# Both heads' exponentials of 512 queries in one instruction, from two-bank score tiles

## The chip, the cores and the metric

The kernel runs on one core of a Trainium2 chip. That core has a matrix engine (TensorE, PE in the profile, with its weight loads listed as PEld), a vector engine (VectorE, DVE), an engine for functions such as the exponential (ScalarE, ACT), a general one (GpSimd, POOL) and SyncE (SP), which here only starts DMAs. The metric is the device time of one execution in microseconds (us). The results of matrix multiplications go to PSUM, a small memory of eight banks; a bank holds 512 float32 numbers in each of 128 partitions. ScalarE and VectorE read the results from there.

## What is computed

Two branches are mixed by a gate: softmax attention with 32 heads of 16 numbers over 2048 positions, and a Fourier mixing made of matrix products.

```python
# x: 2048 x 512
g = sigmoid((x * gate_w).sum(-1, keepdims=True))
q, k, v = (x @ wqkv) split into 32 heads of 16
p = softmax(q @ k.T * 16 ** -0.5)          # per head, 2048 x 2048
a = (p @ v, heads joined) @ wo
b = dft_seq_re @ (x @ dft_hid_re.T) - dft_seq_im @ (x @ dft_hid_im.T)
out = g * a + (1 - g) * b
```

## The kernel before

**The front.** The first part projects x to q, k and v, computes the Fourier branch, and also runs 564 of the 1024 "scans". A scan (`scan`, L110) computes the scores of 128 queries against 512 keys for the two heads of a head pair, and VectorE takes the row maxima of both heads in one reduction (L121). The maxima become a shift that is added inside the score product later, so that the exponentials do not overflow. The front is not touched by the change.

**The attention part** (from L506) works through the 16 head pairs in `NP * PERIODS` = 512 steps, 32 for each pair p. A step takes one block `kb` of 128 keys and one half `h` of the queries (1024 of 2048), and treats it as two score pairs, c = 0 and c = 1, of 512 queries each. The two heads j = 0, 1 of a head pair sit in partitions 0 to 49 and 64 to 113, and their two score products are issued one after the other into different banks, and run beside each other in the two halves of TensorE's rows. I call the two products of c = 0 pair A of a step and those of c = 1 pair B.

`qk2` (L523) does one score pair: it takes a tile `e` in SBUF (six buffers), two PSUM tiles, issues the two products (L530) and then the exponentials (L533) from PSUM into `e`. `pv` (L538) multiplies the four quarters of a step's `e` with the values; its four products write four groups of 32 partitions of the one bank `pvb`, and each appears as two MATMUL records. `pvb` accumulates over 16 steps, is copied out by VectorE (L545), and is divided later on GpSimd (`divide`, L552).

**The order on TensorE** is written out by the loop at L721. In a step n from 1 to 460 it is: pair A of step n; a scan of a later head pair, into the two-bank tile `s1`, which has one buffer; pair B of step n; `pv` of step n-1. TensorE executes this in order, so an instruction that waits holds up all that follows.

The 1024 scans are used up after step 460. From step `MIX` = 461 to 511 the scans' place is taken by the output projection: `outputs()` (L675) hands out pieces of it, one for each step, in tile `s1`, whose accumulated products VectorE adds to the output (`take_in`, L626). In an odd step the piece comes after pair B, and no `pv` is issued; in an even step it comes between pair A and pair B, and then both pending `pv` follow. Two such steps form a cycle: A, B, piece, A, piece, B, `pv`, `pv`. A piece is counted in steps of two products that run beside each other. By the argument of `mix_heads` in L679 the pieces of a cycle have 2 and 2, or 2 and 3, for token blocks 0, 2 and 4 (six cycles), and 4 and 5 for the other thirteen blocks; then `mix_some` (L661) gives three cycles of 3 and 3 and three of 3 and 6. The rest of the output products (L764 to L807) come after step 511, from banks that are taken by `part` (L690) and by `spread` (L772).

**PSUM.** The attention part uses all eight banks: one for `pvb`, two for the tile `s1`, and five single-bank tiles `s2` that `bank()` hands out in rotation. A score product may write a bank when the exponential that read it last is done: with five banks that is the fifth exponential back. An exponential waits for its product; `pv` waits for the exponentials of its step. These waits are semaphores, and the wait of a product stands on its weight load.

Of the kernel before, what the change touches and what calls it, by code (L numbers as in the profile page):

```python
# [10 lines left out]
F32 = mybir.dt.float32  # L11
F32R = mybir.dt.float32r
AF = mybir.ActivationFunctionType
# [5 lines left out]
P = 128  # L19
# [9 lines left out]
SCALE = DH ** -0.5  # L29
# [12 lines left out]
def build(tc, x, xT, wqkv, wo, wrT, wiT, cr, ci, gate, out):  # L42
    nc = tc.nc
    with ExitStack() as ctx:
# [105 lines left out]
        with ExitStack() as pf:  # L150
# [32 lines left out]
            def beside():  # L183

                slots[0] += 1
                run_due()
                if pace[0] is None:
                    return
                pace[1] += 1.0 / pace[0]
                while seen[0] < FRONT and pace[1] >= 1.0:  # L190
                    pace[1] -= 1.0
                    n = seen[0]
                    if n % SCANS == 36:
                        load_scan_beside(n // SCANS + 1)
                    scan(n, s1())
                    seen[0] += 1
                    if seen[0] % SCANS == 0:
                        for d, part in enumerate(shift(n // SCANS)):
                            after(3 + 4 * d, part)
# [234 lines left out]
            with ExitStack() as py:  # L434
# [11 lines left out]
                pss, yre, early = {}, {}, {}  # L446
# [59 lines left out]
        with ExitStack() as pa:  # L506
            ps2 = pa.enter_context(tc.tile_pool(name="ps2", bufs=1, space=PSUM, reuse_waits="tile"))
# [4 lines left out]
            pvb = ps2.tile([P, 512], F32, tag="pv", name="pvb")  # L512
# [4 lines left out]
            def pair_banks():  # L517
                return ps2.tile([P, 2, 512], F32, tag="s1", name="s1")

            def bank():  # L520
                return ps2.tile([P, 512], F32, tag="s2", name="s2", bufs=5)

            def qk2(p, h, kb, c):  # L523
                e = pr.tile([P, 2, 512], F32, tag="e", name="e")
                q0 = h * 1024 + c * 512
                qs, ks = used[p]
                pss = [bank() for j in range(2)]
                for j in range(2):
                    b = 64 * j
                    nc.tensor.matmul(pss[j], ks[b:b + 50, kb * P:(kb + 1) * P],  # L530
                                     qs[b:b + 50, q0:q0 + 512], start=True, stop=True)
                for j in range(2):
                    nc.scalar.activation(e[:, j, :], pss[j], AF.Exp, scale=SCALE)  # L533
                return e

            quads = [(c, j, 64 * c + 32 * j) for c in range(2) for j in range(2)]
# [114 lines left out]
            def mix_rest(t, ps, k, first, last):  # L651

                h, q = t // 8, slice((t % 4) * P, (t % 4 + 1) * P)
                for n, (a, b) in enumerate(((0, 0), (0, 1), (1, 0))):
                    halves_of(ps, direct[h][k][a][:, q], w4[k][b], first and n == 0, last and n == 2)
# [32 lines left out]
            groups = {}  # L688

            def part(t, *ks):  # L690

                if t not in groups:
                    groups[t] = (bank(), pvb) if t == 11 else (bank(), bank())
                    if t in (3, 8):
                        ps = pair_banks()
                        groups[t] = ps[:, 0, :], ps[:, 1, :]
                for k in ks:
                    mix_rest(t, groups[t], k, k == 0 or 7 < t < 11, k == 2)

# [21 lines left out]
            for step in range(NP * PERIODS):  # L721
# [10 lines left out]
                if step in (MIX - 11, (NP - 1) * PERIODS):  # L732
                    for c in range(2):
                        load_y(c + 2 * (step > MIX))
                es = [qk2(p, h, kb, 0)]
                if step == 0:
                    es.append(qk2(p, h, kb, 1))
# [5 lines left out]
                if step:  # L743
                    es.append(qk2(p, h, kb, 1))
                if step >= MIX and step % 2:
                    next(fill)
                if step == NP * PERIODS - 1:
                    part(3, 0)
# [20 lines left out]
            for c in halves_:  # L769
                nc.vector.tensor_copy(ob[:, c], pvb[:, c])  # L770
            part(3, 1)
            spread = [bank(), bank()]  # L772
            for c, ps in zip(halves_, spread):
                nc.tensor.matmul(ps[:, c], sel, ob[:, c], start=True, stop=True)
            part(3, 2)
# [10 lines left out]
            c, ps = halves_[0], spread[0]  # L786
# [8 lines left out]
            c, ps = halves_[1], spread[1]  # L795
# [38 lines left out]
```

## Time and profile before

| | |
|---|---|
| median of 3 runs | 1784.15 us (1782.8 to 1785.89) |
| the profiled execution, its own time | 1785.04 us |
| its span in the trace | 1783.2 us |
| granted clock of TensorE, mean | 0.998 |
| busy share of the span | PE 99%, PEld 58%, DVE 76%, ACT 67%, POOL 44% |
| first exponential of the attention part | 737.1 us |
| steps 0 to 460, with scans | 737.1 to 1640.0 us |
| steps 461 to 511, with pieces of the output | 1640.0 to 1766.1 us |
| the end | 1766.1 to 1783.2 us |

The profile page has sections on the busy time of each engine, on 40 slices of the span, on DMA queues, on the chain of work that ended last, and on groups of instructions. A row of a group reads: line, engine, operation, output<-input, shapes, count | busy time in us, mean ns of one | idle time of the engine before them and what ended it. A row of the timeline reads: start in us, length in us, engine, line, operation, count, and in brackets how long the engine was idle before it and who ended that. Instructions that follow each other directly are joined to one row, so its length is from the first one's start to the last one's end. The length of one instruction is from its dispatch to its completion, and the next one can be dispatched before the first is complete; on a queue that is always full the mean length is therefore more than the distance from one end to the next.

### The profile page before, as it was taken

How to read it: one execution, taken by the hardware profiler on the slowest of the kernel's cores; microseconds unless marked ns; L12 is line 12 of the kernel's file. 1: busy time of each engine (PE TensorE's matmuls, PEld its weight loads, DVE VectorE, ACT ScalarE, POOL GpSimd, SP SyncE). 2: the span in 40 equal slices, each digit the busy share in tenths (PEclk: the TensorE clock that was granted, in tenths of full speed). 3: DMA queues.
4: the chain of work that ended last, by engine and by line, in shares of the span. 5: the costliest groups of instructions: out<-in, count | busy, mean ns of one | idle time of the engine just before them, and what ended most of it. 6: DMA issues, size and time to landing. Idle time of an engine off the chain costs nothing.

```text
span 1783.2 us, 34582 instructions
## 1 busy us (share of the span) xinstructions
PE 1762.2 (99%) x13640; PEld 1033.3 (58%) x13640; DVE 1346.6 (76%) x1296; ACT 1197.1 (67%) x2406; POOL 776.7 (44%) x881
## 2 busy tenths in 40 slices
PE   9999999999999999999999999999999999999998
PEld 7887787877878887544444444444444344444454
DVE  6799999999999999766666666666666666665233
ACT  6445333010020010499999999999999999999885
POOL 3678457666687777322323323232232323323221
PEclk9999999999999999999999999999999999999999
DMA  7663455524565354632351441433332333443512
GB/s 262 217 195 81 123 166 171 128 94 126 159 174 136 126 149 126 120 61 47 57 96 24 82 73 27 94 57 60 61 71 52 68 67 67 86 104 93 135 40 97
DMA packets 119314, 185.85 MB, mean 104 GB/s; under 512 B 53184, under 2 KB 55728, under 8 KB 112240
## 3 DMA queue, kind: packets, MB, share of 16 engines
q1 hardware_dynamic: 77200, 148.96, 32.2%
q0 software_dynamic: 38496, 19.47, 5.3%
q10 hardware_dynamic: 3456, 15.21, 4.0%
q8 instruction: 107, 1.75, 0.4%
q14 instruction: 55, 0.45, 0.1%
HBM read 129.89 MB, written 53.22 MB: 103 GB/s over the span
## 4 chain that ended last, share of the span: by engine, by line
PE 82%; DVE 12%; DMA 1%; issue 1%; POOL 1%; ACT 1%; SPq 0%; DVEq 0%; ACTq 0%; POOLq 0%
PE pvb L540 29%; PE xy L145 21%; PE s L530 19%; PE s L119 11%; DVE mx L121 10%; PE s L145 3%; DMA lc<-ob 1%; POOL s L173 1%; POOL el L173 0%; DVE b L214 0%; DMA abr<-ab_d 0%; DMA raws<-xT 0%; DVE s L173 0%; ACT eh L173 0%; DVE y L627 0%
## 5 line engine op out<-in xcount | busy, mean ns | idle before, releaser
L121 DVE TENSOR_REDUCE mx<-s 128x2 f32<-128x1024 f32 x1024 | 1208.6, 1220 | 303.7 <-PE s L119 303.6
L533 ACT ACTIVATE e<-s 128x512 f32<-128x512 f32 x2048 | 1006.8, 813 | 22.1 <-PE s L530 22.0
L540 PE MATMUL pvb<-e,va 128*17 128x512 f32 x4096 | 553.5, 598 | 0.0
L530 PEld LDWEIGHTS s<-qs,ks 50*128 50x128 f32 x2048 | 263.8, 184 | 437.4 <-issue 412.6
L530 PE MATMUL s<-qs,ks 50*128 50x512 f32 x2048 | 472.9, 450 | 0.0
L119 PE MATMUL s<-ks,qs 48*128 48x512 f32 x2048 | 422.8, 397 | 7.5 <-DVE mx L121 5.2
L496 ACT ACTIVATE tx<-xy,gm 128x512 f32<-128x512 f32 x32 | 22.0, 688 | 380.6 <-PE xy L145 329.7
L119 PEld LDWEIGHTS s<-ks,qs 48*128 48x128 f32 x2048 | 202.3, 185 | 45.2 <-DVE mx L121 18.0
L548 POOL DMA_DIRECT2D lc<-ob x124 | 62.9, 514 | 254.8 <-DVE ob L545 254.6
L540 PEld LDWEIGHTS pvb<-e,va 128*17 128x17 f32 x4096 | 89.6, 95 | 139.5 <-issue 131.7
L555 POOL DMA_DIRECT2D r_d<-lc x31 | 18.1, 582 | 335.0 <-DVE lc L554 335.0
L145 PE MATMUL xy<-w,b 64*128 64x512 f32 x768 | 105.5, 392 | 0.2 <-ACT s L292 0.2
L627 DVE SCALAR_TENSOR_TENSOR y<-s,g,y 128x512 f32<-128x512 f32 x50 | 36.5, 749 | 84.7 <-PE s L145 84.1
L310 ACT ACTIVATE tx<-xy 128x512 f32<-128x512 f32 x48 | 28.7, 598 | 93.6 <-PE xy L145 92.0
L557 POOL DMA_DIRECT2D rb<-r_d x124 | 60.1, 492 | 53.2 <-DMA r_d<-lc 53.0
L145 PEld LDWEIGHTS xy<-w,b 64*128 64x128 f32 x768 | 72.9, 186 | 17.0 <-ACT s L292 0.7
L558 POOL TENSOR_TENSOR ob<-ob,rb 128x512 f32<-128x512 f32 x31 | 39.7, 1281 | 70.4 <-DMA rb<-r_d 70.4
L408 POOL TENSOR_TENSOR ab<-tx,ty 128x512 f32<-128x512 f32 x32 | 41.3, 1290 | 50.7 <-ACT ty L311 32.2
L173 POOL TENSOR_TENSOR el<-s,eh 128x512 fp32r<-128x512 f32 x32 | 41.9, 1310 | 48.5 <-ACT eh L173 37.0
L173 ACT CAST eh<-s 128x512 fp32r<-128x512 f32 x32 | 19.9, 621 | 41.2 <-POOL s L173 28.9
L450 POOL TENSOR_TENSOR y<-tx,ty 128x512 f32<-128x512 f32 x32 | 41.7, 1303 | 7.0 <-DVE ty L498 7.0
L145 PE MATMUL xy<-b,w 64*128 64x512 f32 x336 | 43.4, 390 | 0.5 <-DVE b L214 0.5
(925 smaller groups left out, 2005.0 us busy)
## 6 DMA issues: line engine op xcount, KB each, us to landing
craw<-ci SPq DMA_DIRECT2D x64, 256.0 KB
craw<-cr SPq DMA_DIRECT2D x60, 256.0 KB
ks<-k_d SPq DMA_DIRECT2D x48, 256.0 KB
qs<-q_d SPq DMA_DIRECT2D x48, 256.0 KB
ab_d<-ab SPq DMA_DIRECT2D x32, 256.0 KB
y_d<-y SPq DMA_DIRECT2D x32, 256.0 KB
o_d<-oh POOLq DMA_DIRECT2D x28, 256.0 KB, 9.4
o_d<-ol POOLq DMA_DIRECT2D x28, 256.0 KB, 14.3
```

What stands on the lines that cost most here:

```text
L119: nc.tensor.matmul(ps[:, j, :], qs[b:b + 48, qb * P:(qb + 1) * P], ks[b:b + 48, c * 512:(c + 1) * 512], start=True, stop=True)
L121: nc.vector.tensor_reduce(mx[p][:, :, qb, c], ps, axis=AX.X, op=ALU.max)
L145: nc.tensor.matmul(ps[j], lhs[r], rhs[r], start=first, stop=last)
L173: d[2](*d[3])
L408: nc.gpsimd.tensor_add(ab, tx, ty)
L450: nc.gpsimd.tensor_add(y, tx, ty)
L530: nc.tensor.matmul(pss[j], ks[b:b + 50, kb * P:(kb + 1) * P], qs[b:b + 50, q0:q0 + 512], start=True, stop=True)
L533: nc.scalar.activation(e[:, j, :], pss[j], AF.Exp, scale=SCALE)
L540: nc.tensor.matmul(pvb[r:r + VC, :], va[:, kb, 2 * p + j, :], es[c][:, j, :], start=kb == 0, stop=kb == NB - 1, tile_position=(0, r))
L548: nc.gpsimd.dma_start(lc[32 * n:32 * n + 32, :], ob[r + DH:r + VC, :].rearrange("p (s e) -> p s e", e=16))
L557: nc.gpsimd.dma_start(rb[r:r + DH, :], r_d[p][h][n:n + 1, :].to_broadcast([DH, 512]))
L558: nc.gpsimd.tensor_mul(ob, ob, rb)
```

## The change

`qk2` takes one tile of two neighbouring banks (`bank2`, tag `s3`, two buffers) in place of two single banks, and one ACTIVATE of 128 x 1024 in place of two of 128 x 512. The five `s2` banks become one `s2` bank and the two `s3` tiles, so eight banks are still in use. At the end `part` and `spread` take their banks from the new tiles: token blocks 8 and 10 from `s3`, block 9 (in place of 8) from `s1`, block 11 the single `s2` bank beside `pvb`.

```diff
             def bank():
-                return ps2.tile([P, 512], F32, tag="s2", name="s2", bufs=5)
+                return ps2.tile([P, 512], F32, tag="s2", name="s2")
+
+            def bank2():
+                ps = ps2.tile([P, 2, 512], F32, tag="s3", name="s3", bufs=2)
+                return ps, (ps[:, 0, :], ps[:, 1, :])
 
             def qk2(p, h, kb, c):
                 e = pr.tile([P, 2, 512], F32, tag="e", name="e")
                 q0 = h * 1024 + c * 512
                 qs, ks = used[p]
-                pss = [bank() for j in range(2)]
+                ps, pss = bank2()
                 for j in range(2):
                     b = 64 * j
                     nc.tensor.matmul(pss[j], ks[b:b + 50, kb * P:(kb + 1) * P],
                                      qs[b:b + 50, q0:q0 + 512], start=True, stop=True)
-                for j in range(2):
-                    nc.scalar.activation(e[:, j, :], pss[j], AF.Exp, scale=SCALE)
+                nc.scalar.activation(e, ps, AF.Exp, scale=SCALE)
                 return e
...
                 if t not in groups:
-                    groups[t] = (bank(), pvb) if t == 11 else (bank(), bank())
-                    if t in (3, 8):
+                    if t in (3, 9):
                         ps = pair_banks()
                         groups[t] = ps[:, 0, :], ps[:, 1, :]
+                    else:
+                        groups[t] = (bank(), pvb) if t == 11 else bank2()[1]
...
             part(3, 1)
-            spread = [bank(), bank()]
+            spread = bank2()[1]
```

In the order of instructions that the two programs are built to, TensorE's sequence is the same in both, step for step. ScalarE issues 1024 exponentials in place of 2048. In the program before, a product waits for ScalarE bank by bank; in the program after, the first product of each pair waits for the exponential of the pair before last, and `pv` has no wait of its own left in the steps 1 to 460.

## The prediction

> **What bounds the kernel now.** I read the slices of the span first, then the groups of ScalarE, then single steps of the timeline. From the page:
>
> ```profile
> PE   9999999999999999999999999999999999999998
> ACT  6445333010020010499999999999999999999885
> ...
> PE 82%; DVE 12%; DMA 1%; issue 1%; POOL 1%; ACT 1%; SPq 0%; DVEq 0%; ACTq 0%; POOLq 0%
> ```
>
> The chain of waits gives TensorE 82% and ScalarE 1%. But in the attention part, from the 18th slice on, ScalarE's row is full too, and a chain that steps back along an engine that shows no idle time stays on that engine. So I ask for ScalarE's groups while scans run (737 to 1640 us), and for the stages (columns of the second view: window, its length, busy us and instructions of PE, PEld, DVE, ACT and POOL, granted clock, DMA share, GB/s):
>
> ```profile
> L533 ACT ACTIVATE e<-s 128x512 f32<-128x512 f32 x1841 | 902.7, 832 | 1.0 <-PE s L530 0.8
> ```
>
> ```profile
> 737.10:1640.00 902.90, 900.38 (x6432) 374.66 (x6432) 597.69 (x562) 901.93 (x1842) 261.13 (x391) 1.00 0.35 67
> 1640.00:1766.10 126.10, 126.10 (x1013) 66.76 (x1012) 36.09 (x52) 104.87 (x209) 27.06 (x41) 1.00 0.33 85
> ```
>
> 1841 exponentials in 902.7 us, with 1.0 us idle: one each 0.490 us, four a step, 1.96 us a step, and 902.9 us for 461 steps. In this stage ScalarE sets the pace. The other two engines are close behind, as one step shows (timeline):
>
> ```profile
> 988.22 0.19 PEld L530 LDWEIGHTS s<-qs,ks 50*128 50x128 f32 x2 [0.85 <-issue]
> 988.22 0.50 PE L530 MATMUL s<-qs,ks 50*128 50x512 f32 x2
> 988.33 0.19 PEld L119 LDWEIGHTS s<-ks,qs 48*128 48x128 f32 x2
> 988.56 0.40 PE L119 MATMUL s<-ks,qs 48*128 48x512 f32 x2
> 988.80 0.43 PE L530 MATMUL s<-qs,ks 50*128 50x512 f32 x2
> 989.00 1.23 DVE L121 TENSOR_REDUCE mx<-s 128x2 f32<-128x1024 f32 x1 [0.73 <-PE s L119]
> 989.16 1.09 PE L540 MATMUL pvb<-e,va 128*17 128x512 f32 x8
> ...
> 990.18 0.50 PE L530 MATMUL s<-qs,ks 50*128 50x512 f32 x2
> 990.29 0.19 PEld L119 LDWEIGHTS s<-ks,qs 48*128 48x128 f32 x2
> ...
> 990.52 0.40 PE L119 MATMUL s<-ks,qs 48*128 48x512 f32 x2
> ```
>
> The scan's own loop: product at 988.56, reduction 989.00 to 990.23, weight load of the next scan 990.29, next product 990.52, which is 1.96 us. The tile `s1` has one buffer, so this loop can't be much under 1.96, whatever ScalarE does. TensorE goes A at 988.22, scan at 988.56, B at 988.80, `pv` at 989.16, A again at 990.18.
>
> **What the change removes.** One ACTIVATE out of two. The merged one's cost is not in the trace; the slope is, in ScalarE's groups of other sizes:
>
> ```profile
> L381 ACT ACTIVATE xg<-xg 128x512 f32<-128x512 f32 x16 | 10.1, 633 | 0.0
> L213 ACT CAST b<-raws 128x512 fp32r<-128x512 f32 x16 | 9.8, 619 | 4.2 <-DMA raws<-xT 4.2
> L213 ACT CAST w<-raws 128x256 fp32r<-128x256 f32 x8 | 3.2, 402 | 0.0
> L395 ACT ACTIVATE z<-z 128x16 f32<-128x16 f32 x1 | 0.2, 216 | 0.0
> ```
>
> From 16 to 512 elements: 417 ns for 496, so 0.430 us for 512 more. The casts give 2 x 217 = 0.434, the lowest pairing (16 to 256) 0.397, and the top is 0.490, nothing saved. I take 0.43, the one from an ACTIVATE. Back to back, a merged exponential then costs 0.49 + 0.43 = 0.92 us, and ScalarE needs 1.84 a step, 0.12 less than now. That gain has no taker, because the scan loop stands at 1.96.
>
> **What the change adds: a longer wait for banks.** Before, a pair needs the exponentials four and five back; ScalarE always has a backlog. After, pair B of step n needs the exponential of pair B of step n-1, the very last one issued before step n, whole. And A, B and `pv` are in order on TensorE: behind a waiting B stand `pv` of step n-1 and pair A of step n+1, whose exponential ScalarE wants next. That closes a loop:
>
> end of exponential B(n-1) -> pair B(n) -> `pv` -> pair A(n+1) -> exponential A(n+1) -> exponential B(n+1), two steps later.
>
> The last stage of the kernel (two cycles, with ScalarE not full) shows each link without queueing:
>
> ```profile
> 1655.62 0.30 PEld L530 LDWEIGHTS s<-qs,ks 50*128 50x128 f32 x4 [0.85 <-issue]
> ...
> 1656.21 0.60 ACT L533 ACTIVATE e<-s 128x512 f32<-128x512 f32 x1 [1.04 <-PE s L530]
> ...
> 1656.86 0.18 PEld L530 LDWEIGHTS s<-qs,ks 50*128 50x128 f32 x1 [0.25 <-ACT e L533]
> ...
> 1657.84 0.18 PEld L530 LDWEIGHTS s<-qs,ks 50*128 50x128 f32 x1 [0.31 <-ACT e L533]
> 1658.27 0.13 PEld L540 LDWEIGHTS pvb<-e,va 128*17 128x17 f32 x8 [0.25 <-issue]
> ...
> 1659.14 0.12 PEld L540 LDWEIGHTS pvb<-e,va 128*17 128x17 f32 x4 [0.31 <-issue]
> 1660.11 0.19 PEld L530 LDWEIGHTS s<-qs,ks 50*128 50x128 f32 x2 [0.85 <-issue]
> 1660.12 0.50 PE L530 MATMUL s<-qs,ks 50*128 50x512 f32 x2
> ```
>
> ```profile
> 1660.71 4.03 ACT L533 ACTIVATE e<-s 128x512 f32<-128x512 f32 x8 [0.47 <-PE s L530]
> ```
>
> - end of an exponential (1656.21 + 0.60) to the load that waited for it (1656.86): 0.05;
> - a score product that waited, to `pv` (1657.84 to 1658.27): 0.43;
> - `pv` to the next pair A: two in 1.84 (1658.27 to 1660.11), the second 0.87 after the first, so 0.97 alone; the steady step has 1.02, with `pv` held by the last exponential. After the change nothing holds it: 0.98;
> - pair A: 0.50; its end (1660.62) to the exponential's dispatch (1660.71): 0.09;
> - an exponential that finds ScalarE idle: 0.60 now, 0.60 + 0.43 = 1.03 merged;
> - the one behind it ends 0.49 later now ((4.03 - 0.60) / 7), 0.92 merged.
>
> Sum: 0.05 + 0.43 + 0.98 + 0.50 + 0.09 + 1.03 + 0.92 = 4.00 us for two steps, **2.00 us a step**. TensorE's own work between two pairs A is 0.34 to the scan, 0.24 to B, 0.36 to `pv` and 0.98, together 1.92, so it now idles 0.08 a step in front of pair B; ScalarE idles 0.16. Before, the same loop counts 0.05 + 0.98 + 0.50 + 0.09 + 0.60 + 3 x 0.49 = 3.69 for two steps (it enters at `pv`'s last quarter), hidden under ScalarE's 3.92. VectorE's copy of `pvb`, each 16 steps, stays at nothing:
>
> ```profile
> 990.37 0.69 DVE L545 COPY ob<-pvb 128x512 f32<-128x512 f32 x1
> ...
> 991.12 0.17 PEld L540 LDWEIGHTS pvb<-e,va 128*17 128x17 f32 x8 [0.25 <-DVE ob L545]
> ```
>
> Its `pv` starts 0.94 after pair A (990.18 to 991.12), as in the step without a copy (988.22 to 989.16): A, scan and B cover it. Without that cover it would cost 0.69, 29 times, 20 us.
>
> The scan stage: 461 x (2.00 - 1.96) = **+18.4 us**.
>
> **The last stage.** A cycle with pieces of 4 and 5:
>
> ```profile
> 1693.86 0.30 PEld L530 LDWEIGHTS s<-qs,ks 50*128 50x128 f32 x4 [0.85 <-issue]
> ...
> 1695.13 0.19 PEld L530 LDWEIGHTS s<-qs,ks 50*128 50x128 f32 x2
> ...
> 1695.60 1.32 PE L145 MATMUL s<-wo,oc 64*128 64x512 f32 x10
> ...
> 1698.92 0.19 PEld L530 LDWEIGHTS s<-qs,ks 50*128 50x128 f32 x2 [0.85 <-issue]
> ```
>
> The second A loads 1.27 after the first, and the piece behind it starts at 1.74. After the change that A needs the first A's merged exponential: 0.50 + 0.09 + 1.03 + 0.05 = 1.67; the next product starts 0.34 after a load that waited (988.22 to 988.56), at 2.01. So +0.27, 13 times: 3.5 us. In cycles with short pieces the second B sets the pace. Now it waits for the third exponential of the cycle (1657.84, 2.22 after 1655.62), after it for the second merged one: 1.67 + 0.92 = 2.59. So +0.37, nine times (2 and 2, 2 and 3, 3 and 3): 3.3 us. With 3 and 6 the second A decides, at 1.24 now (1656.86) and 1.67 after: +0.43, three times, 1.3 us. Together **+8.1 us**.
>
> The new banks at the end (blocks 8 to 11, `spread`) keep TensorE's order; I put them at 0. They come in the last 17.1 us, where the waits are for the last division, in the same place before and after; if block 9's `s1` tile were late by the length of one product, that is 0.4 us.
>
> **The sum**: 18.4 + 8.1 = 26.5 on the profiled execution's 1785.0, its span of 1783.2 and 1.8 around it: 1811.5. That execution lies 0.9 over the median of the runs, so 1811.
>
> The Trainium skill ("ScalarE: Activation LUTs", section "What ACT_TABLE_LOAD costs") gives an ACTIVATE with immediates 186 ns + 0.833 N, of which 93 overlap with the next: for N = 512 that is 613 and 520, against 0.60 and 0.49 in the rows above. By it the merged pair would take 1.04 and 0.95, the loop 4.04, and the time would be some 10 us more than my sum; I stay with the rows.
>
> **The rivals.** *The waits stay hidden* (12%). If pair B's wait were covered, the step would be held by the scan loop alone. Its rows give 1.96 with an error of about 0.02, so 0 to -0.02 a step: 1776 to 1785, about 1781 with the last stage covered too. For it speaks that ScalarE is saturated now and needs 0.12 less; against it, that TensorE has only 2.00 - 1.92 = 0.08 of slack in my loop, and none against the exponential's end.
> The Trainium skill ("Perfetto Trace Analysis", section "Optimizing Scalar/DVE Operations") says that grouping raises throughput on a saturated engine, and that, where ScalarE isn't saturated but causes bubbles on other engines, breaking instructions up can let work finish sooner: the first is this rival, the second my forecast.
>
> *A merged exponential costs as much as two* (10%): 0.49 in place of 0.43 for the second half. Both ScalarE links grow by 0.06, the step is 2.06, +46 us; the last stage +10: 1841. Against it: all slopes above lie under 0.44.
>
> *A pair that waited pays the full load* (7%): the 0.43 was seen with one of two products waiting. With load to product 0.23 (990.29 to 990.52) and B to `pv` 0.36 the link is 0.59, the loop 4.16, the step 2.08: +55 and +10, 1850.
>
> **How the numbers follow.** My forecast has 71%. Its own range goes from a slope of 0.397 (1.967 a step, -15 in the scan stage: 1796) to links that are 0.03 a step longer in all (+14: 1825). Range: 1795 to 1842, up to the rival of a merged exponential without a saving; it leaves out the hidden waits and the full load, 19%. Slower by over 0.2% (3.6 us, about what can be told from no change here) are 71 + 10 + 7, less 3 for a forecast whose gaps are smaller than they look: 0.85. The hidden case splits into 0.06 faster and 0.06 same, and with those 3 the chance of same is 0.09.
>
> **What would show it.** Right: steps of 2.00 us between 737 and about 1658 us; pair B's weight load with idle time ended by the exponential, TensorE idle about 0.08 there; the merged ACTIVATE 1.03 long where it finds ScalarE idle; ScalarE under 95% busy in the stage; the last stage about 134 us. Wrong: steps of 1.96 or less with ScalarE idle and waits on VectorE's reduction (the first rival), or an ACTIVATE over 1.07 long.

## The result, and the profile after

The kernel after takes 1815.04 us, the median of 4 runs (1813.23 to 1816.64), against 1784.28 of 4 runs of the kernel before (1782.8 to 1785.89). The ratio is 1.017, with a 95% interval of 1.0154 to 1.019: slower by 31 us, where the forecast was 27. The profiled execution of after took 1814.87 us, with a span of 1813.0.

First, the stages. The view of windows gives for each stretch its length, then busy us and instructions of PE, PEld, DVE, ACT and POOL, the granted clock, and the DMA share and rate. The borders are the first exponential of step 0, that of step 461, the end of the last exponential, and the end. In the kernel before, the first exponential of step 461 is at 1641.9; the border of 1640.0 in the table ahead of the prediction is a step too early. Before:

```profile
737.10:1641.90 904.80, 902.28 (x6444) 375.26 (x6444) 598.73 (x564) 903.83 (x1845) 262.89 (x393) 1.00 0.35 67
1641.90:1766.00 124.10, 124.10 (x997) 66.15 (x999) 35.05 (x50) 102.93 (x205) 25.31 (x39) 1.00 0.34 86
1766.00:1783.20 17.20, 8.92 (x60) 4.91 (x54) 10.62 (x14) 2.59 (x6) 4.84 (x4) 0.88 0.41 153
```

After:

```profile
736.90:1661.90 925.00, 922.91 (x6442) 296.06 (x6442) 597.89 (x564) 884.00 (x923) 264.65 (x395) 1.00 0.35 65
1661.90:1794.10 132.20, 127.90 (x996) 61.07 (x998) 35.05 (x50) 98.04 (x103) 23.47 (x37) 1.00 0.31 81
1794.10:1813.00 18.90, 8.94 (x60) 4.88 (x56) 11.80 (x14) 2.69 (x6) 4.53 (x4) 0.92 0.38 140
```

| stage | before | after | difference | forecast |
|---|---|---|---|---|
| front | 737.1 | 736.9 | -0.2 | 0 |
| steps 0 to 460, with scans | 904.8 | 925.0 | +20.2 | +18.4 |
| steps 461 to 511 | 124.1 | 132.2 | +8.1 | +8.1 |
| the end | 17.2 | 18.9 | +1.7 | 0 |

The last stage came out as the sum had it, the scan stage 1.8 us longer; the end was put at nothing and grew. In the scan stage ScalarE was busy without a gap before (903.8 of 904.8 us) and isn't after (884.0 of 925.0). TensorE's busy time is over 99% of the stage in both, so it doesn't show the wait; the idle time of its weight loads does. The row of before (737 to 1640 us) and that of after (737 to 1660 us), total us, times, longest:

```profile
PEld s L530 <- issue: 390.5, 459, 0.9
```

```profile
PEld s L534 <- ACT e L536: 510.2, 909, 0.9
```

Before, once in a step the score's weight load had idle time in front of it, and nothing that the profile shows ended it. After, it has that twice in a step, and by the profile an exponential ended it each time. For pair B that is so, as the next rows show; for pair A the exponential named had ended earlier, and what held the load was `pv` ahead of it on TensorE. (The 510 us aren't a loss: the weight loads are idle during every `pv`, 0.85 us of it in a step.)

The loop itself, from the timeline of after. Pair A's loads are those with 0.85 idle, pair B's the others:

```profile
987.67 0.19 PEld L534 LDWEIGHTS s<-qs,ks 50*128 50x128 f32 x2 [0.85 <-ACT e L536]
...
988.28 1.02 ACT L536 ACTIVATE e<-s 128x1024 f32<-128x1024 f32 x1
...
988.38 0.19 PEld L534 LDWEIGHTS s<-qs,ks 50*128 50x128 f32 x2 [0.35 <-ACT e L536]
...
988.80 0.13 PEld L543 LDWEIGHTS pvb<-e,va 128*17 128x17 f32 x8 [0.24 <-issue]
...
989.79 0.18 PEld L534 LDWEIGHTS s<-qs,ks 50*128 50x128 f32 x2 [0.85 <-ACT e L536]
989.79 0.50 PE L534 MATMUL s<-qs,ks 50*128 50x512 f32 x2
...
990.36 0.41 PE L534 MATMUL s<-qs,ks 50*128 50x512 f32 x2
...
990.39 2.92 ACT L536 ACTIVATE e<-s 128x1024 f32<-128x1024 f32 x3 [0.18 <-PE s L534]
...
991.68 0.19 PEld L534 LDWEIGHTS s<-qs,ks 50*128 50x128 f32 x2 [0.85 <-ACT e L536]
...
992.38 0.18 PEld L534 LDWEIGHTS s<-qs,ks 50*128 50x128 f32 x2 [0.35 <-ACT e L536]
```

Pair B's load is released at 988.38, 0.05 after the end of pair B's exponential of the step before (the same 0.05 in all but one of the steps 2 to 459 of this trace); `pv` follows 0.42 later, pair A 0.99 after that; A's product ends at 990.29, and its exponential is dispatched at 990.39, with ScalarE idle for 0.18 before it. Two exponentials later, at 992.38, the next but one pair B is released: 4.00 us for two steps. The steps are not equal (987.67, 989.79, 991.68: 2.12 and 1.89), which a loop that closes only over two steps allows. Pair A's load at 989.79 needs the exponential dispatched at 988.28, which ended at 989.30, half a microsecond before. In the short step pair B's product comes 0.57 after pair A's load (989.79 to 990.36), as in the kernel before (0.58), so TensorE is held up only in every second step, by about 0.23 (2.12 against 1.89).

### The profile page after: what moved, and what is told of

Same layout as the page of the kernel before. It is cut to its first block, busy times and chain, and to the rows that moved or that the text cites. A ratio compares the mean times of both kernels' runs of the same rounds, so it can differ in the third digit from the quotient of the medians.

```text
span 1813.0 us, 34078 instructions
## 1 busy us (share of the span) xinstructions
PE 1785.8 (98%) x13640; PEld 956.8 (53%) x13640; DVE 1347.9 (74%) x1296; ACT 1172.6 (65%) x1382; POOL 775.4 (43%) x881
## 4 chain that ended last, share of the span: by engine, by line
PE 83%; DVE 12%; DMA 1%; ACT 1%; issue 1%; POOL 1%; SPq 0%; DVEq 0%; ACTq 0%; POOLq 0%
PE pvb L543 28%; PE s L534 22%; PE xy L145 20%; PE s L119 11%; DVE mx L121 10%; PE s L145 2%; ACT e L536 1%; POOL s L173 1%; POOL el L173 0%; DVE b L214 0%; DMA abr<-ab_d 0%; DMA q_d<-eh 0%; DMA raws<-xT 0%; DMA raws<-wqkv 0%; DVE y L630 0%
## 5 line engine op out<-in xcount | busy, mean ns | idle before, releaser
L536 ACT ACTIVATE e<-s 128x1024 f32<-128x1024 f32 x1024 | 982.1, 1022 | 75.2 <-PE s L534 72.3
L543 PE MATMUL pvb<-e,va 128*17 128x512 f32 x4096 | 534.3, 598 | 0.0
L534 PE MATMUL s<-qs,ks 50*128 50x512 f32 x2048 | 482.8, 471 | 4.4 <-ACT e L536 4.0
L534 PEld LDWEIGHTS s<-qs,ks 50*128 50x128 f32 x2048 | 189.1, 183 | 552.1 <-ACT e L536 549.2
L543 PEld LDWEIGHTS pvb<-e,va 128*17 128x17 f32 x4096 | 70.6, 95 | 137.9 <-issue 130.5
```

What stands on the lines that cost most here:

```text
L536: nc.scalar.activation(e, ps, AF.Exp, scale=SCALE)
L543: nc.tensor.matmul(pvb[r:r + VC, :], va[:, kb, 2 * p + j, :], es[c][:, j, :], start=kb == 0, stop=kb == NB - 1, tile_position=(0, r))
```

## Experiments

Each was run once beside the kernel before on the same chip, the last one four times.

### The merge undone, the two-bank tiles kept

```diff
-                nc.scalar.activation(e, ps, AF.Exp, scale=SCALE)
+                for j in range(2):
+                    nc.scalar.activation(e[:, j, :], pss[j], AF.Exp, scale=SCALE)
```

> The changed kernel with its two-bank tiles kept and only the merge undone: two exponentials of 512 each. My theory: the loss comes from having two pairs of banks, and the merge itself gains. The loop over two steps then has four exponentials in it, 0.60 + 3 x 0.49 = 2.07 us, in place of 1.03 + 0.92 = 1.95, so a step is 2.06 us and the time about 1843 us, slower than the changed kernel. Rival (the merged exponential is what costs, because pv and the next pair get their data and banks later): undoing it brings the time back towards 1785, and under 1815 in any case.

Measured: 1851.1 us. The loop, from weight loads of pair B that an exponential released (timeline of this run):

```profile
999.87 0.19 PEld L534 LDWEIGHTS s<-qs,ks 50*128 50x128 f32 x2 [0.28 <-ACT e L537]
...
1002.01 0.19 PEld L534 LDWEIGHTS s<-qs,ks 50*128 50x128 f32 x2 [0.44 <-ACT e L537]
...
1004.00 0.18 PEld L534 LDWEIGHTS s<-qs,ks 50*128 50x128 f32 x2 [0.28 <-ACT e L537]
```

4.13 us for two steps, where the loop with four exponentials has 4.12. So the two parts of the change have opposite signs: going from five banks to two tiles of two costs about 65 us (1786 to 1851), and the merge gives back 36 of them (1851 to 1815). The rival, that merging costs, falls. My 1843 was 8 us too low: the scan stage has 2.08 us a step on average (958.4 us for 461), where I had 2.06. What this run does not show is how much of the 65 us comes from the lost fifth bank and how much from two banks coming free together; no run has four single banks.

### Only pair A merged, pair B on three single banks

```diff
-                return ps2.tile([P, 512], F32, tag="s2", name="s2")
+                return ps2.tile([P, 512], F32, tag="s2", name="s2", bufs=3)
...
-                ps = ps2.tile([P, 2, 512], F32, tag="s3", name="s3", bufs=2)
+                ps = ps2.tile([P, 2, 512], F32, tag="s3", name="s3")
...
-                ps, pss = bank2()
+                ps, pss = (None, (bank(), bank())) if c else bank2()
...
-                nc.scalar.activation(e, ps, AF.Exp, scale=SCALE)
+                if c:
+                    for j in range(2):
+                        nc.scalar.activation(e[:, j, :], pss[j], AF.Exp, scale=SCALE)
+                else:
+                    nc.scalar.activation(e, ps, AF.Exp, scale=SCALE)
```

At the end, `part` and `spread` take their banks as far as possible as in the kernel before.

> Pair A keeps a merged exponential from one two-bank tile, pair B has two exponentials from three single banks, so that pair B no longer waits for the exponential just before it but for the third back. My theory: the loop is opened (it falls to about 1.8 us a step), ScalarE needs 1.90, TensorE 1.92, the scan's loop 1.95 to 1.96: 1.95 a step, the scan stage -5 us against before, the last stage +6, so about 1786 us (1780 to 1792). Rival (merging costs by itself, half as many merges cost half): about 1800 us.

Measured: 1764.3 us, against 1786.4 of before on the same chip: faster by 22 us, where I had expected no change. The loop is open, as the theory says, but the next bound was misjudged. The windows of this run's scan stage, and its scan in the timeline:

```profile
735.30:1613.60 878.30, 875.65 (x6445) 329.47 (x6446) 598.73 (x564) 875.24 (x1385) 262.60 (x393) 1.00 0.35 69
```

```profile
1001.05 0.19 PEld L534 LDWEIGHTS s<-qs,ks 50*128 50x128 f32 x2 [0.85 <-ACT e L540]
...
1001.23 0.18 PEld L119 LDWEIGHTS s<-ks,qs 48*128 48x128 f32 x2
1001.39 0.40 PE L119 MATMUL s<-ks,qs 48*128 48x512 f32 x2
...
1001.83 1.23 DVE L121 TENSOR_REDUCE mx<-s 128x2 f32<-128x1024 f32 x1 [0.65 <-PE s L119]
...
1003.11 0.36 PEld L119 LDWEIGHTS s<-ks,qs 48*128 48x128 f32 x2
1003.28 0.51 PE L119 MATMUL s<-ks,qs 48*128 48x512 f32 x2
```

ScalarE is full again (875.2 of 878.3 us), at 878.3 / 461 = 1.905 us a step, what one merged and two single exponentials need (0.92 + 0.98). The scan's loop goes round in 1.89 (1001.39 to 1003.28), so it wasn't held at 1.96 by its own links. In both kernels the scan's product comes 0.34 after pair A's load (1001.05 to 1001.39 here, 988.22 to 988.56 before). Its own load comes 0.18 after pair A's here and came 0.11 after it before, so that the product followed its load after 0.16 here and after 0.23 there: part of the 0.23 was a wait behind pair A.

### Without scans, two tiles

```diff
-                scan(n, pair_banks())
+                if n % SCANS == 0:
+                    mx[n // SCANS] = sm.tile([P, 2, NB, 4], F32, tag="mx", name="mx")
+                nc.vector.memset(mx[n // SCANS][:, :, n % SCANS // 4, n % 4], 120.0)
```

> The changed kernel without the scans of steps 0 to 460: their products and reductions are left out, and a small memset sets the row maxima to a constant. My theory: the scan is not a link of the loop that sets 2.00 us a step, so the step stays at 2.00 although TensorE has 0.24 us and VectorE 1.2 us less to do; time 1810 to 1818 us. Rival (the step is set by the scan's loop or by TensorE being full): the step falls to TensorE's 1.68 or ScalarE's 1.84, the time to 1740 us or less.

Measured: 1813.1 us. With 460 scans less to do, the stage has the same length:

```profile
735.50:1660.20 924.70, 872.01 (x5522) 232.48 (x5522) 48.18 (x564) 880.52 (x923) 264.83 (x395) 1.00 0.35 68
```

VectorE's work falls from 597.9 to 48.2 us and the stage stays at 925. Neither the scan nor the amount of work on TensorE or VectorE sets the step of after. That leaves the loop, which the next run opens.

### Without scans, three tiles

The change is the one above, and until step 460 `bank2` hands out three two-bank tiles in rotation, the third being the scans' tile `s1`.

```diff
+                tags = ("s1", "s3", "s5") if now[0] < MIX else ("s3", "s5")
+                turn[0] += 1
-                ps = ps2.tile([P, 2, 512], F32, tag="s3", name="s3", bufs=2)
+                ps = ps2.tile([P, 2, 512], F32, tag=tags[turn[0] % len(tags)], name="s3")
```

> As the run without scans, and the two banks that the scans had serve the score pairs as a third two-bank tile until step 460. The same work is left out. My theory: with three tiles nothing waits for the exponential just before, ScalarE alone sets the pace with 2 x 0.92 = 1.84 us a step; the scan stage is 848 us in place of 925, the time about 1738 us. Rival (something other than the number of tiles holds a step at 2.00): the time stays over 1800 us.

Measured: 1735.0 us. ScalarE's groups in the scan stage:

```profile
L540 ACT ACTIVATE e<-s 128x1024 f32<-128x1024 f32 x920 | 843.4, 1111 | 0.0
```

843.4 / 920 = 0.917 us for a merged exponential with no idle time at all: the merge's full saving, and all that it lacked, without scans, was a third tile. (With scans the eight banks have no room for one.) Against the run with two tiles, one more tile is worth 78 us.

### The kernel before, without scans

> The kernel before, without the scans of steps 0 to 460 (products and reductions left out, a small memset in their place). My theory: ScalarE's four exponentials of 0.49 us set the step of 1.96 us before the change, not the scan's loop, so the time stays within 1778 to 1788 us. Rival (the scan's loop, which I read as 1.96 us, set the step): it falls to what the loop over the banks allows, about 1.85 us a step, and the time to about 1735 us.

The edit is the one of the two runs above, on the kernel before. Measured: 1785.4 us, against 1785.05 of before. ScalarE's row of the scan stage:

```profile
L533 ACT ACTIVATE e<-s 128x512 f32<-128x512 f32 x1840 | 902.0, 839 | 2.0 <-PE s L530 2.0
```

0.490 us each, with and without scans. So the reading of what bound the kernel before was right. The run above differs from this one in the merge and in its banks, and ScalarE is full in both, so the difference is the merge's saving: 1785.4 to 1735.0 is 50 us. In the scan stage alone it is about 60 (905.6 to 845.0 us); the last stage and the end of that run, which has two tiles again there, lose 10.

### Two tiles for spread

```diff
-            spread = bank2()[1]
+            spread = [bank2()[1][0] for c in range(2)]
```

> The changed kernel with the two halves of spread in two different two-bank tiles in place of the two banks of one. Theory: the end grew from 17.1 to 18.9 us because the first reciprocal waits for both halves of one tile, and the products after it then fall together with GpSimd's additions; with two tiles the end is 17.0 to 17.5 us again and the rest unchanged. Rival (blocks 8 and 9 in other banks made the end longer): it stays at 18.5 us or more.

Measured: 1815.3 us as a whole, but the end in its windows is as short as before:

```profile
1796.30:1813.40 17.10, 8.90 (x60) 4.94 (x56) 10.60 (x14) 2.57 (x6) 4.84 (x4) 0.92 0.42 154
```

The gain of 1.8 us doesn't show in the time because this run's scan stage was 2.9 us longer (927.85) and its front only 0.7 shorter. VectorE's rows of the end, before, after, and with two tiles:

```profile
1768.73 1.76 DVE L787 RECIPROCAL rb<-s 128x256 f32<-128x256 f32 x1 [0.75 <-issue]
1770.53 0.43 DVE L788 TENSOR_TENSOR ob<-ob,rb 128x256 f32<-128x256 f32 x1
```

```profile
1797.26 1.76 DVE L791 RECIPROCAL rb<-s 128x256 f32<-128x256 f32 x1 [1.17 <-issue]
1799.06 1.42 DVE L792 TENSOR_TENSOR ob<-ob,rb 128x256 f32<-128x256 f32 x1
```

```profile
1799.02 1.76 DVE L791 RECIPROCAL rb<-s 128x256 f32<-128x256 f32 x1 [0.74 <-issue]
1800.81 0.42 DVE L792 TENSOR_TENSOR ob<-ob,rb 128x256 f32<-128x256 f32 x1
```

In one tile the reciprocal of the first half waits for both halves' products (1.17 idle against 0.75). The product after it then falls together with GpSimd's addition and takes 1.42 in place of 0.43. With two tiles both are back, and blocks 8 and 9 are where they were in the kernel after, so the rival falls.

### Pair A merged until step 460, five single banks from step 461

The PSUM pool of the score banks is closed at step 461 and opened again with five single banks; the exponentials are split from there on, and the end takes its banks as in the kernel before.

```diff
-                pss = [bank() for j in range(2)]
+                merged = now[0] < MIX and c == 0
+                if merged:
+                    ps = hold.pool.tile([P, 2, 512], F32, tag="s3", name="s3")
+                    pss = ps[:, 0, :], ps[:, 1, :]
+                else:
+                    pss = [bank() for j in range(2)]
...
+                if step == MIX:
+                    banks("scores5", 5)
```

> Until step 460 as the mixed kernel (pair A merged from one two-bank tile, pair B split over three banks), and from step 461 on the five single banks and split exponentials of the kernel before. Theory: the scan stage is the mixed kernel's 878 us, the last stage 124 us as before, the end 17.1 us: with the front 737 + 878 + 124 + 17 + 2 = 1758 us (1754 to 1762). Rival (the last stage is longer in the mixed kernel for another reason than its banks): it stays at 1764 us.

Measured: 1758.1 us, the median of 4 runs (1757.27 to 1759.74), against 1785.05 of 6 runs of before; the ratio is 0.985, with a 95% interval of 0.9832 to 0.9867. Its stages:

```profile
737.00:1615.80 878.80, 876.05 (x6444) 330.01 (x6444) 598.68 (x564) 875.59 (x1384) 262.37 (x393) 1.00 0.35 69
1615.80:1739.70 123.90, 123.90 (x997) 65.92 (x1000) 35.03 (x50) 102.89 (x205) 25.81 (x39) 1.00 0.33 86
```

This version beats both: the scan stage of the mixed kernel and the last stage of the kernel before, without a loss between. From step 461 on it has both the single banks and the split exponentials back, so by itself it doesn't say which of them cost the 8 us. The run with the merge undone and the tiles kept does; its last stage is

```profile
1695.70:1830.30 134.60, 128.45 (x997) 61.06 (x1000) 35.13 (x50) 104.38 (x204) 23.14 (x36) 1.00 0.30 79
```

134.6 us with the tiles alone, against 132.2 with tiles and merge and 124.1 with neither: here too the tiles cost and the merge gives a little back.

## Why the prediction was right, point by point

- **ScalarE sets the pace before**: shown. Without scans the kernel before keeps its 0.490 us an exponential and its time.
- **The cost of a merged exponential**: 1.03 forecast where ScalarE is idle, 1.02 measured (a mean of 1022 ns in the group's row of after); 0.92 forecast back to back, 0.917 measured. Per 512 elements more that is 0.42 (1.02 against 0.60) and 0.427 (0.917 against 0.490). The row of its profile page:

```profile
L536 ACT ACTIVATE e<-s 128x1024 f32<-128x1024 f32 x1024 | 982.1, 1022 | 75.2 <-PE s L534 72.3
```

  The Trainium skill ("ScalarE: Activation LUTs", section "What ACT_TABLE_LOAD costs") has 0.833 ns an element, which is 0.427 for 512. The slope agrees with these rows; its fixed part of 186 ns does not, since 1022 less 853 for 1024 elements leaves 169.
- **The loop**: shown. Its 4.00 us for two steps were forecast and measured; with four exponentials in it, it has 4.13; it doesn't move when the scans are left out; without scans, it vanishes with a third tile. TensorE's wait was forecast as 0.08 in each step; it came as about 0.23 in every second one. The stage came out 1.8 us longer than the sum: the step is 2.007 after and 1.963 before (925.0 / 461 and 904.8 / 461), where the sum had 2.00 and 1.96.
- **The last stage**: shown. The forecast put the second A's load 1.67 after the first and the piece behind it at 2.01. The timeline of after has

```profile
1712.10 0.30 PEld L534 LDWEIGHTS s<-qs,ks 50*128 50x128 f32 x4 [0.85 <-ACT e L536]
...
1713.78 0.18 PEld L534 LDWEIGHTS s<-qs,ks 50*128 50x128 f32 x2 [0.45 <-ACT e L536]
...
1714.12 1.32 PE L145 MATMUL s<-wo,oc 64*128 64x512 f32 x10
```

  1.68 and 2.02. Over the 25 cycles of the stage, from the first pair A's load to the next cycle's, the usual length went from 5.07 to 5.35 us with pieces of 4 and 5, from 4.49 to 4.88 in the nine with short pieces, and from 5.13 to 5.56 with 3 and 6: +0.28, +0.39 and +0.43, where the forecast had +0.27, +0.37 and +0.43. So the sum of 8.1 is no luck of terms that cancel. (The sign of "about 134 us" counted from 1640.0; from the first exponential of step 461 the stage is 132.2.)
- **The end at 0**: the term that was mis-sized; it measured 1.7 us. I looked at TensorE's order, which is unchanged, and not at what the reciprocal waits for when two banks become one tile.
- **"This loop can't be much under 1.96, whatever ScalarE does"**: wrong, and with it "that gain has no taker". The scan's loop runs in 1.89 in the mixed kernel. I had added up links from a step in which other things were close behind each other, and took a load's wait behind pair A as a link of the scan's own. TensorE's own 1.92 a step was too long as well, since the mixed kernel's step is 1.905 and the short step of after 1.89. The forecast did not rest on either, but the rival of hidden waits did: its price of 1781 should have been lower, as the 1764 and 1758 of the two mixed kernels show.
- **The sign of ScalarE's busy share**: I named "under 95%" as what would show the theory right; the windows have 95.6% (884.0 of 925.0). The time of one exponential is its 1.02 from dispatch to completion, of which 0.1 can overlap with the one before. By 0.917 each, ScalarE works 1.83 of 2.01 us, 91%.

The Trainium skill says that larger operations can help a saturated engine, and that smaller ones may help where an engine that isn't saturated makes others wait ("Perfetto Trace Analysis", section "Optimizing Scalar/DVE Operations"). The first is borne out: 50 us gained without scans, where ScalarE is saturated. The second, which the prediction set beside its forecast, isn't: in the kernel after, ScalarE isn't saturated and TensorE waits for it, yet breaking its instructions up in the same tiles cost 36 us. What lost the 31 us is the banks that the merge needs, not the length of its instruction.

## What to carry to other kernels

Merging instructions on a saturated engine saves their fixed part, but the merged one needs its inputs in one larger buffer and holds them as long as all of its parts together. Count how many results back the producer has to wait, in instructions of the new size, and walk the whole loop from release to release: here a wait for the fourth and fifth instruction back became one for the second back, of double size, and that turned an in-order queue into a chain. Where buffers are short, merging only a part can win more than merging all; and a loop's links are to be read where it really waits, not summed from a step in which other queues touch it.

## What the runs showed of the hardware

An operation of VectorE on two SBUF tiles, 128 x 256, takes 0.42 us with GpSimd idle. When an addition of GpSimd had started shortly before, it took 1.42 and 1.07 (all rows from the end of after; the first product is shown above):

```profile
1798.92 1.27 POOL L786 TENSOR_TENSOR y<-y,take 128x512 f32<-128x512 f32 x1 [28.37 <-ACT take L785]
...
1801.68 1.29 POOL L786 TENSOR_TENSOR y<-y,take 128x512 f32<-128x512 f32 x1
...
1802.18 1.07 DVE L801 TENSOR_TENSOR ob<-ob,rb 128x256 f32<-128x256 f32 x1
...
1803.72 0.42 DVE L803 TENSOR_TENSOR ol<-ob,oh 128x256 fp32r<-128x256 f32 x1 [0.47 <-ACT oh L802]
```

The first addition ended at 1800.19 and VectorE's product at 1800.48; the second ended at 1802.97 and the product at 1803.25. Both times VectorE was done 0.28 to 0.29 after GpSimd, however long it had been waiting. The Trainium skill ("SBUF — State Buffer", section "Who interferes with whom") says that a VectorE instruction with two SBUF inputs contends with a GpSimd instruction that reads SBUF, and that who issues first holds the shared pair of ports; the trace agrees.

The second thing is how exactly a wait repeats: a score product that an exponential released was followed by `pv` after 0.42 to 0.43 us in the kernel before (the last stage), in after and in the run with split exponentials (999.87 to 1000.29). In the last two, pair A's load came 0.98 to 0.99 later (1000.29 to 1001.27 in the split run).
